# The x products on 64 by 64 tiles of TensorE, with heads and w_in rows rearranged, in a linear attention + snake MLP kernel

## The chip, the cores and the metric

The program runs on one NeuronCore of one Trainium2 chip. The metric is device time in microseconds (us), the median of three runs. One run under the profiler shows where the time lies. PE is TensorE (its weight loads are shown apart as PEld), DVE is VectorE, ACT is ScalarE, POOL is GpSimd, SP is SyncE, which issues most transfers. Times in the text without a unit are us.

## The reference

Eight batches, 8 heads, 576 positions, head size 64. Per batch and head:

```
q_s = softmax(q over its 64 columns)       k_s = softmax(k over the 576 positions)
kv  = k_s^T v          (64 x 64)
x   = q_s kv           (576 x 64), heads side by side: x is 4608 x 512
h   = x w_in           (4608 x 2048)
g   = h + sin(alpha h)^2 / alpha
out = g w_out          (4608 x 512)
```

Inputs and output are float32; all products run in bfloat16 with float32 sums in PSUM.

## The kernel before, in words

**Layouts.** A position of a batch is p*9 + j with 64 values p and J = 9 values j, and a column block (b, j) is 64 positions wide. Heads sit as h = 2i + e: i is 0 to 3 (i = 2*ii + x), e is 0 or 1. `ke` and `vb` hold e on the partition half; `qT` (transposed softmaxed q) holds for each ii the two heads x on the two partition halves. The kv product (`kv_mm`, line 174) is already made of 64 by 64 pieces: 64 rows of the array by 64 columns, 72 matmuls of 65 columns a batch (the 65th column is the softmax sum), which leaves heads x on the partition halves of PSUM tile `kvp`. `kv_norm` (184 to 188) divides by the sum and writes `kbd`, a 128 by 128 block diagonal matrix for each (e, ii) with zeros off the diagonal: two DVE instructions, one for each half.

**x products.** x is made transposed, as `xT`: 4 chunks of 128 rows by a ring of 2560 columns. One full 128 by 128 matmul with `kbd` (lines 223 and 231) makes one chunk c = 2*ii + e, of which only the diagonal blocks do work. So a batch takes 4 chunks times 576 columns.

**The MLP.** The 4608 columns are cut into 9 tiles t of 512. `mm_h` (254) makes the first product for 128 of the 2048 hidden rows at a time (16 blocks ni, 4 matmuls of 512 columns each); `sine` (260, 262 or 264, 266) squares the sine on ACT, POOL or DVE; `combine` (270, DVE) writes g. `mm_o` (274) is the second product: 4 row groups j of 16 matmuls of 512 columns, each group evacuated by DVE (286) and stored.

**PSUM.** Eight banks: two rotating `a`, two rotating `b`; later a pool `ps_o` of two and `ps_a` of two adjoining banks (one tile, for kv and x). A tile's first products use `aabb` four times over.

**Order.** It is written out by hand, engine by engine; every engine runs its own instructions in the order of the program. Tiles 0 to 2 have orders of their own (lines 361 to 595). In tiles 3 to 6 the batch b = t + 1 is prepared: ACT starts the tile with four exponentials of b (with a table load before and after), 8 second products of tile t - 1 go to PE, and then for each ni: `mm_h`, at ni = 3 the transposes by DMA and the loads of batch b + 1 on SP's queue, at ni = 5 the kv product, at ni = 9, 11, 13, 15 one pair of x products each into `ps_a` with one DVE copy each, then sine, combine and so many second products of tile t - 1 that `want` is reached. Tiles 7 and 8 interleave four second products with each block.

Of the kernel before, what the change touches and what calls it, by code (L numbers as in the profile page):

```python
# [15 lines left out]
F32 = mybir.dt.float32  # L16
# [7 lines left out]
def kernel(  # L24
# [20 lines left out]
    J = 9  # L45
# [26 lines left out]
    alpha_rows = singles.tile([nN, 128], F32, name="alpha_rows")  # L72
    alpha_sb = singles.tile([128, nN], F32, name="alpha_sb")
    inva_sb = singles.tile([128, nN], F32, name="inva_sb")
    kbd = [singles.tile([128, 2, 2, 128], BF16, name=f"kbd{n}") for n in range(2)]
    vb = [singles.tile([128, J, 4 * 65], BF16, name=f"vb{n}") for n in range(2)]

    def src_view(t, b):
        return t[b].rearrange("(i e) (p j) d -> (e p) i (j d)", e=2, j=J)

    win_v = moe_w_in.rearrange("(x c d) n -> x d c n", x=2, c=4)
    wout_v = moe_w_out.rearrange("(no ni) d -> ni no d", ni=128)
    out_v = out.rearrange("(b p j) d -> b j p d", b=B, j=J)

# [94 lines left out]
    def kv_norm(b, i0=0, i1=2):  # L179

        kt, m = kbd[b % 2], i1 - i0
        kvr = small.tile([128, 2, 2], F32, name="kvr")[:, :, 0:m]
        src = A["kvp", b][:, :, i0 * 65:i1 * 65].rearrange("p e (ii c) -> p e ii c", ii=m)
        nc.vector.reciprocal(kvr, src[:, :, :, D])
        for x in range(2):
            r = slice(64 * x, 64 * x + 64)
            nc.vector.tensor_tensor(kt[r, :, i0:i1, r], src[r, :, :, 0:D],  # L187
                                    kvr[r].unsqueeze(3).to_broadcast([64, 2, m, D]), op=ALU.mult)

    def q_tile(b):  # L190
        if ("qT", b) not in A:
# [23 lines left out]
    XO = ((0, 4), (4, 9))  # L215

    def attn_out(b, ii, half, pool, eng):
        qT, kt = A["qT", b], kbd[b % 2]
        j0, j1 = XO[half]
        n = (j1 - j0) * P  # L220
        xp = pool.tile([128, 2, 512], F32, name="xp", tag="a")
        for e in range(2):
            nc.tensor.matmul(xp[:, e, 0:n], kt[:, e, ii], qT[:, ii, j0:j1, e * 64:(e + 1) * 64],  # L223
                             start=True, stop=True)
        c0 = (J * b + j0) * P % NX
        eng(xT[:, 2 * ii:2 * ii + 2, c0:c0 + n], xp[:, :, 0:n])  # L226

    def attn_chunk(b, c, j0, j1, xp):

        ii, e = divmod(c, 2)  # L230
        nc.tensor.matmul(xp, kbd[b % 2][:, e, ii], A["qT", b][:, ii, j0:j1, e * 64:(e + 1) * 64],
                         start=True, stop=True)


    G = {}

    HP = {}
    BANKS = {0: "aabbkllaabbkllaa", 1: "kbbllaakbbllaabb", 2: "aabbooaabbooaabb"}

    def bank(kind):  # L240

        if kind == "k":
            return ps_k.tile([128, 2, MF], F32, name="kvp", tag="a")[:, 0]
        pool = {"a": lambda: ps_h[0], "b": lambda: ps_h[1], "l": lambda: ps_l, "o": lambda: ps_o}[kind]()
        return pool.tile([128, MF], F32, name={"l": "lp", "o": "op"}.get(kind, "hp"), tag=kind)

    def mm_h(t, ni, k0=0, k1=4):

        if ni == 0 and k0 == 0:
            G[t] = gpool.tile([128, nN, MF], BF16, name="g")  # L250
        hp = HP[t, ni] if k0 else bank(BANKS.get(t, 4 * "aabb")[ni])
        HP[t, ni] = hp
        for ki in range(k0, k1):
            nc.tensor.matmul(hp, win[:, ki, ni * 128:(ni + 1) * 128],  # L254
                             xT[:, ki, t * MF % NX:t * MF % NX + MF], start=(ki == 0), stop=(ki == 3))
        return hp

    def sine(t, ni, hp, sq):
# [48 lines left out]
    zero = singles.tile([128, 1], F32, name="zero")  # L307
    nc.vector.memset(zero, 0.0)
    for n in range(2):
        nc.vector.memset(kbd[n], 0.0)  # L310
        nc.vector.memset(vb[n].rearrange("p j (i c) -> p j i c", i=4)[:, :, :, D:D + 1], 1.0)

    ps_h = [ctx.enter_context(tc.tile_pool(name=f"ps_{n}", bufs=2, space=PSUM, reuse_waits="tile")) for n in "ab"]
# [63 lines left out]
    kv_norm(0, 0, 1)  # L377
    tp1 = ps_l.tile([128, 8, 128], BF16, name="tp", tag="l")
    q_transpose_ii(0, 1, 0, 8, tp1)
    cast_v0(1, 0, 5, ACT_CP)  # L380
    cast_v0(1, 5, 9, DVE_CP)

    xp = [bank("b") for _ in range(2)]
    for c in range(2):
        attn_chunk(0, c, 0, 8, xp[c])
    DVE_CP(xT[:, 0, 0:MF], xp[0])
    ACT_CP(xT[:, 1, 0:MF], xp[1])
    ACT_CP(A["qT", 0][:, 1, 0:8], tp1)
    nc.scalar.activation(zero, zero, AX.Sin)
    kv_mm(0, 1, ps_k, split=True)  # L390
# [1 line left out]
    for ki in range(2):  # L392
        for ni in range(2):
            mm_h(0, ni, ki, ki + 1)
    for c in range(2, 4):
        xp = bank("l")
        attn_chunk(0, c, 0, 8, xp)
        DVE_CP(xT[:, c, 0:MF], xp)
    for ki in range(2):
        for ni in range(2, 4):  # L400
            mm_h(0, ni, ki, ki + 1)
# [21 lines left out]
    def take(it, n=1000):  # L423
        for _ in range(n):
            if next(it, 0) == 0:
                return
# [4 lines left out]
    with ES:  # L431
# [47 lines left out]

        def x_half(ii):  # L480
            xp = [bank("a") for _ in range(2)]
            for e in range(2):
                attn_chunk(1, 2 * ii + e, 0, 8, xp[e])
            for e in range(2):
                (ACT_CP, DVE_CP)[e](xT[:, 2 * ii + e, MF:2 * MF], xp[e])

        kv_mm(1, 0, ps_k, split=True)
        kv_norm(1, 0, 1)
# [23 lines left out]
        def late_q8(ni):  # L512
            if ni == 11:
                tp = ps_k.tile([128, 2, 2, 128], BF16, name="tp", tag="a")
                for b in range(2):
                    for ii in range(2):
                        nc.tensor.transpose(tp[:, ii, b], A["qe", 1][:, J - 2 + b, ii * 128:(ii + 1) * 128], identb)
                DVE_CP(A["qT", 1][:, :, J - 2:J], tp)
            elif ni == 15:
                xp = ps_k.tile([128, 4, 2, P], F32, name="xp", tag="a")  # L520
                for c in range(4):
                    ii, e = divmod(c, 2)
                    for b in range(2):
                        nc.tensor.matmul(xp[:, c, b], kbd[b][:, e, ii],
                                         A["qT", 1][:, ii, J - 2 + b, e * 64:(e + 1) * 64], start=True, stop=True)
                DVE_CP(xT[:, :, 16 * P:18 * P], xp.rearrange("p c b n -> p c (b n)"))

        for ni in range(nN):
            h_slot(1, ni, SQ[ni], lag)
# [2 lines left out]
        cast_v(2, [GP_CP, GP_CP])  # L532
        flush(lag, 0)

    ps_o = ctx.enter_context(tc.tile_pool(name="ps_o", bufs=2, space=PSUM, reuse_waits="tile"))
    ps_a = ctx.enter_context(tc.tile_pool(name="ps_a", bufs=1, space=PSUM, reuse_waits="tile"))


    def o_stream(t, eng=DVE_CP):
        for j in range(4):  # L540
            acc = ps_o.tile([128, dm], F32, name="op", tag="o")
# [21 lines left out]
    norm_q(3, [GP])  # L563
    take(os, 20)

    c0 = J * 2 * P
    for c in range(4):
        xp = bank("aabb"[c])[:, 0:6 * P]
        attn_chunk(2, c, 0, 6, xp)
        (ACT_CP, DVE_CP)[c % 2](xT[:, c, c0:c0 + 6 * P], xp)  # L570
        take(os, 3 if c == 1 else 1)
    xp = ps_a.tile([128, 2, 512], F32, name="xp", tag="a")[:, :, 0:6 * P]
    for c in range(4):
        attn_chunk(2, c, 6, 9, xp[:, c // 2, (c % 2) * 3 * P:(c % 2 + 1) * 3 * P])
    DVE_CP(xT[:, :, c0 + 6 * P:c0 + 9 * P].rearrange("p (h c) n -> p h c n", h=2),
           xp.rearrange("p h (c n) -> p h c n", c=2))
    take(os)
    q_transpose_dma(3)
    load_batch(4)

    def attn_back(b, n, engs=4 * (DVE_CP,), xs=(4, 6, 8, 10)):
        if n == 0:
            kv_mm(b, 0, ps_a)
            kv_mm(b, 1, ps_a)
            kv_norm(b)
        elif n in xs:
            m = xs.index(n)
            attn_out(b, m // 2, m % 2, ps_a, engs[m])

    SQ2 = "PAPPAPAPPAPAPPAP"  # L590
    for ni in range(nN):
        h_slot(2, ni, SQ2[ni], lag)
        flush(lag, 2)
        attn_back(3, ni - 5, (DVE_CP, ACT_CP, ACT_CP, DVE_CP), (4, 6, 8, 10))
    flush(lag, 0)

    for t in range(3, nT):
        b = t + 1 if t + 1 < B else None
        os = o_stream(t - 1)
        done = 0  # L600
# [58 lines left out]
```

## Time and profile before

| | |
|---|---|
| median of 3 runs | 284.34 (284.31 to 284.47) |
| the profiled execution, its own time | 283.85 |
| its span, first to last instruction | 282.1 |
| granted PE clock, mean | 0.997 |
| PE busy | 270.1 (96%) |
| ACT busy | 225.5 (80%) |
| DVE busy | 188.7 (67%) |
| POOL busy | 83.8 (30%) |
| DMA | 45.80 MB, mean 162 GB/s |

A matmul's row shows its latency (379 ns for 512 columns); matmuls overlap, and in a stream they start 0.2157 apart (16 of them take 3.45 in the chain of waits). In the tables "idle before" is time in which the engine had nothing to run before a group, and behind the arrow stands what ended it. Some matmul records are missing from a trace: where a hole of one whole step stands in a regular stream, it is a missing record.

### The profile page before, as it was taken

The page shows a single profiled execution, that of the slowest core. Times are in us where ns is not written, and L with a number is a line of the kernel's source. Part 1 is how long each engine was busy: PE and PEld are TensorE (multiplying, and loading weights), DVE is VectorE, ACT ScalarE, POOL GpSimd, SP SyncE. Part 2 cuts the span into 40 slices and gives each one's busy share as a digit, 9 for nine tenths or more (in the row PEclk, how much of TensorE's full clock was granted, in tenths as well). Part 3 has the DMA queues.
Part 4 walks back from the last instruction along what each step waited for, and adds up shares of the span by engine and source line. Part 5 has one row for each costly group of instructions (what it writes and reads, how often), then busy time and mean ns, then how long its engine had stood idle before and what let it go on. Part 6 is the DMA issues. An engine that isn't in the chain of part 4 may idle for free.

```text
span 282.1 us, 4812 instructions
## 1 busy us (share of the span) xinstructions
PE 270.1 (96%) x1826; PEld 128.0 (45%) x1855; DVE 188.7 (67%) x288; ACT 225.5 (80%) x322; POOL 83.8 (30%) x80
## 2 busy tenths in 40 slices
PE   1999999999999999999999999999999999999994
PEld 0444444444444444444444444444444444444443
DVE  3968768899967768766875677567775555555412
ACT  3989576999589999899989998999877777777400
POOL 1988421877676550115003500340000000000000
PEclk9999999999999999999999999999999999999998
DMA  7999999996599039811992099109011111111143
GB/s 252 310 173 221 280 332 322 358 345 243 124 224 393 10 68 329 305 37 38 266 386 50 22 283 388 27 18 160 6 34 37 37 40 37 37 38 43 42 104 74
DMA packets 39127, 45.80 MB, mean 162 GB/s; under 512 B 17072, under 2 KB 22464, under 8 KB 39104
## 3 DMA queue, kind: packets, MB, share of 16 engines
q1 hardware_dynamic: 33360, 40.57, 46.9%
q0 software_dynamic: 5552, 4.79, 10.4%
q8 instruction: 14, 0.23, 0.3%
q10 hardware_dynamic: 192, 0.14, 0.2%
q14 instruction: 9, 0.07, 0.1%
HBM read 36.71 MB, written 9.44 MB: 164 GB/s over the span
## 4 chain that ended last, share of the span: by engine, by line
PE 84%; DMA 6%; ACT 3%; DVE 2%; POOL 1%; issue 1%; SPq 1%; ACTq 0%
PE op L274 38%; PE hp L254 37%; DMA st_v<-in_v_dram 6%; PE xp L223 2%; PE kvp L174 2%; PE lp L254 2%; POOL s L264 1%; PE op L629 1%; PE op L254 1%; ACT s L260 1%; PE kvp L254 1%; ACT vb L329 1%; DVE g L270 1%; SPq L299 1%; SPq L445 0%
## 5 line engine op out<-in xcount | busy, mean ns | idle before, releaser
L270 DVE SCALAR_TENSOR_TENSOR g<-s,inva_sb,hp 128x512 bf16<-128x512 f32 x128 | 94.1, 745 | 58.1 <-ACT s L262 52.6
L254 PE MATMUL hp<-xT,win 128*128 128x512 bf16 x507 | 127.9, 379 | 0.4
L274 PE MATMUL op<-wout,g 128*128 128x512 bf16 x477 | 121.6, 379 | 1.4 <-issue 0.6
L260 ACT ACTIVATE s<-hp,alpha_sb 128x512 f32<-128x512 f32 x128 | 86.3, 682 | 22.9 <-PE hp L254 21.2
L254 PEld LDWEIGHTS <-win 128*128 128x128 bf16 x576 | 56.0, 98 | 67.5 <-issue 1.3
L274 PEld LDWEIGHTS <-g 128*128 128x128 bf16 x560 | 54.0, 98 | 61.0 <-DVE g L270 0.3
L262 ACT ACTIVATE s<-s 128x512 f32<-128x512 f32 x112 | 70.5, 630 | 3.5
L264 POOL TENSOR_TENSOR s<-s 128x512 f32<-128x512 f32 x29 | 30.4, 1063 | 20.0 <-ACT s L260 19.9
L153 POOL TENSOR_TENSOR qn<-qe,qs 128x1152 bf16<-128x1152 bf16 (+1 forms) x12 | 25.1, 2109 | 34.1 <-DVE qs L147 22.7
L286 DVE COPY o<-op 128x512 f32<-128x512 f32 (+2 forms) x33 | 22.1, 668 | 9.9 <-PE op L274 5.5
L138 POOL CAST vb<-st_v 128x1152 bf16<-128x1152 f32 x12 | 14.7, 1257 | 45.3 <-DMA st_v<-in_v_dram 45.3
L119 ACT ACTIVATE qe<-st_q 128x1152 bf16<-128x1152 f32 (+2 forms) x18 | 17.7, 1025 | 6.7 <-DMA st_q<-in_q_dram 6.6
L119 ACT ACTIVATE ke<-st_k 128x1152 bf16<-128x1152 f32 x16 | 17.9, 1151 | 1.2 <-DMA st_k<-in_k_dram 1.2
L146 DVE TENSOR_REDUCE qs<-qe 128x36 f32<-128x2304 bf16 x5 | 12.8, 2553 | 7.9 <-ACT qe L119 7.9
L226 DVE CAST xT<-xp 128x512 bf16<-128x512 f32 (+1 forms) x18 | 13.5, 749 | 0.0
L119 ACT ACT_TABLE_LOAD x7 | 9.0, 1283 | 1.3 <-PEq L643 1.2
L274 PE MATMUL lp<-wout,g 128*128 128x512 bf16 x31 | 8.8, 379 | 0.2 <-issue 0.2
L274 PE MATMUL hp<-wout,g 128*128 128x512 bf16 x30 | 8.6, 379 | 0.1
L223 PE MATMUL xp<-qT,kbd 128*128 128x256 bf16 (+1 forms) x40 | 8.2, 286 | 0.0
L174 PEld LDWEIGHTS <-ke 64*64 64x64 bf16 x576 | 5.8, 108 | 4.6 <-ACT ke L119 0.8
L187 DVE TENSOR_TENSOR kbd<-kvp,kvr 64x256 bf16<-64x256 f32 (+1 forms) x20 | 7.4, 369 | 0.5
L254 PE MATMUL lp<-xT,win 128*128 128x512 bf16 x30 | 7.5, 379 | 0.1
(86 smaller groups left out, 135.0 us busy)
## 6 DMA issues: line engine op xcount, KB each, us to landing
out_dram<-o SPq DMA_DIRECT2D x70, 128.0 KB, 2.4
st_q<-in_q_dram SPq DMA_DIRECT2D x6, 1152.0 KB, 6.7
st_k<-in_k_dram SPq DMA_DIRECT2D x6, 1152.0 KB, 8.8
st_v<-in_v_dram SPq DMA_DIRECT2D x6, 1152.0 KB, 11.4
st_k<-in_k_dram SPq DMA_DIRECT2D x4, 576.0 KB, 7.5
st_q<-in_q_dram SPq DMA_DIRECT2D x4, 512.0 KB, 6.1
st_v<-in_v_dram SPq DMA_DIRECT2D x3, 576.0 KB, 8.0
wout<-in_moe_w_out_dram POOLq DMA_DIRECT2D x3, 512.0 KB, 10.3
```

Source lines behind the costliest of these rows:

```text
L119: nc.scalar.activation(dst[:, :, ii * 128:(ii + 1) * 128].rearrange("p j (x d) -> p x j d", x=2), src[:, ii::2], AX.Exp)
L138: engs[ii](vv[:, 2 * ii:2 * ii + 2, :, 0:D], staged["v", b][:, ii::2])
L153: engs[ii % len(engs)].tensor_tensor(qn[:, ii, 0:j1].rearrange("p j (x d) -> p j x d", x=2), qe[:, ii], part.unsqueeze(3).to_broadcast([12 ...
L223: nc.tensor.matmul(xp[:, e, 0:n], kt[:, e, ii], qT[:, ii, j0:j1, e * 64:(e + 1) * 64], start=True, stop=True)
L226: eng(xT[:, 2 * ii:2 * ii + 2, c0:c0 + n], xp[:, :, 0:n])
L254: nc.tensor.matmul(hp, win[:, ki, ni * 128:(ni + 1) * 128], xT[:, ki, t * MF % NX:t * MF % NX + MF], start=(ki == 0), stop=(ki == 3))
L260: nc.scalar.activation(s, hp, AX.Sin, scale=alpha_sb[:, ni:ni + 1])
L262: nc.scalar.activation(s, s, AX.Square)
L264: nc.gpsimd.tensor_tensor(s, s, s, op=ALU.mult)
L270: nc.vector.scalar_tensor_tensor(G[t][:, ni], in0=s, scalar=inva_sb[:, ni:ni + 1], in1=hp, op0=ALU.mult, op1=ALU.add)
L274: nc.tensor.matmul(acc, G[t][:, ni, j * 128:(j + 1) * 128], wout[:, ni, :], start=(ni == 0), stop=(ni == nN - 1))
L286: eng(o[:, cols], acc)
```

## The change

1. `kbd` keeps the 64 by 64 blocks alone, without zeros: `kv_norm` needs one DVE instruction on 128 partitions instead of two on 64, and the two clearing instructions at the start fall away.
2. An x product is four matmuls on 64 by 64 tiles (row half x, column half e) in place of two full ones. A chunk of `xT` now holds the two heads e of one (x, ii): chunk 2x + ii. Rows of w_in are permuted to match by the view that loads them, and `mm_h` runs over the chunks in the order 0, 2, 1, 3.
3. A batch's first 8 column blocks go as 512 columns; the ninth (`last_j`) goes apart: for batches 3 to 6 inside the next batch's kv product, in spare columns of its PSUM tile.
4. Batches 4 to 7: all x products at ni = 12 in one group, on four banks (one of `a`, one of `ps_o`, the two of `ps_a`), with copies at ni = 12, 13 and 14. For batch 3 two groups, at ni = 9 and 13, all copies on DVE. `ps_o` becomes two pools of one bank, and blocks 12 to 15 of a tile go `abba`.
5. In tiles 3 to 6, 17 second products instead of 8 go ahead of block 0, and `want` follows another line.
6. At the start ACT and DVE swap their parts of one cast of v.

```diff
-    kbd = [singles.tile([128, 2, 2, 128], BF16, name=f"kbd{n}") for n in range(2)]
+    kbd = [singles.tile([128, 2, 2, D], BF16, name=f"kbd{n}") for n in range(2)]
...
-    win_v = moe_w_in.rearrange("(x c d) n -> x d c n", x=2, c=4)
+    win_v = moe_w_in.rearrange("(c x d) n -> x d c n", x=2, c=4)
...
-        for x in range(2):
-            r = slice(64 * x, 64 * x + 64)
-            nc.vector.tensor_tensor(kt[r, :, i0:i1, r], src[r, :, :, 0:D],
-                                    kvr[r].unsqueeze(3).to_broadcast([64, 2, m, D]), op=ALU.mult)
+        nc.vector.tensor_tensor(kt[:, :, i0:i1], src[:, :, :, 0:D],
+                                kvr.unsqueeze(3).to_broadcast([128, 2, m, D]), op=ALU.mult)
...
+    def attn_x(b, ii, j0, j1, outs):
+
         for e in range(2):
-            nc.tensor.matmul(xp[:, e, 0:n], kt[:, e, ii], qT[:, ii, j0:j1, e * 64:(e + 1) * 64],
-                             start=True, stop=True)
+            for x in range(2):
+                r = slice(64 * x, 64 * x + 64)
+                nc.tensor.matmul(outs[x][64 * e:64 * e + 64], kbd[b % 2][r, e, ii],
+                                 A["qT", b][r, ii, j0:j1, e * 64:(e + 1) * 64], start=True, stop=True)
...
+    def x_copy(eng, c, b, xp):
+
+        n0 = min(8 * P, NX - J * b * P % NX)
+        for n, m in ((0, n0), (n0, 8 * P)):
+            if n < m:
+                d0 = (J * b * P + n) % NX
+                eng(xT[:, c, d0:d0 + m - n], xp[..., n:m])
+
+    def last_j(b, xn):
+
+        for ii in range(2):
+            attn_x(b, ii, J - 1, J, [xn[:, x, ii * P:(ii + 1) * P] for x in range(2)])
...
+    KO = (0, 2, 1, 3)
...
-        hp = HP[t, ni] if k0 else bank(BANKS.get(t, 4 * "aabb")[ni])
+        hp = HP[t, ni] if k0 else bank(BANKS.get(t, 3 * "aabb" + "abba")[ni])
...
-        nc.vector.memset(kbd[n], 0.0)
...
-    cast_v0(1, 0, 5, ACT_CP)
-    cast_v0(1, 5, 9, DVE_CP)
+    cast_v0(1, 0, 5, DVE_CP)
+    cast_v0(1, 5, 9, ACT_CP)
...
-    ps_o = ctx.enter_context(tc.tile_pool(name="ps_o", bufs=2, space=PSUM, reuse_waits="tile"))
+    ps_o = [ctx.enter_context(tc.tile_pool(name=f"ps_{n}", bufs=1, space=PSUM, reuse_waits="tile")) for n in "op"]
...
+    for ii in range(2):
+        xp = [bank("ab"[ii]) for _ in range(2)]
+        attn_x(2, ii, 0, 8, xp)
+        if ii == 1:
+            xn = ps_a.tile([128, 2, 512], F32, name="xp", tag="a")
+            last_j(2, xn)
+        for x in range(2):
+            x_copy((ACT_CP, DVE_CP)[x], 2 * x + ii, 2, xp[x])
+        take(os, 4)
+    last_j_copy(2, xn)
...
+    def x_pair(b, ii):
+        xp = ps_a.tile([128, 2, 512], F32, name="xp", tag="a")
+        attn_x(b, ii, 0, 8, [xp[:, x] for x in range(2)])
+        return xp
+
+    def attn_kv(b):
+
+        kv_mm(b, 0, ps_a)
+        kv_mm(b, 1, ps_a)
+        if b > 3:
+            xn = A["kvp", b][:, :, 256:512]
+            last_j(b - 1, xn)
+        kv_norm(b)
+        if b > 3:
+            last_j_copy(b - 1, xn)
...
-        attn_back(3, ni - 5, (DVE_CP, ACT_CP, ACT_CP, DVE_CP), (4, 6, 8, 10))
+        if ni == 5:
+            attn_kv(3)
+        elif ni in (9, 13):
+            ii = ni // 12
+            x_copy(DVE_CP, slice(ii, 4, 2), 3, x_pair(3, ii))
...
-            take(os, 8)
-            done = 8
+            take(os, 17)
+            done = 17
...
-                attn_back(b, ni - 5)
+                if ni == 5:
+                    attn_kv(b)
+                elif ni == 12:
+                    xl = [bank("a"), bank("o")]
+                    attn_x(b, 1, 0, 8, xl)
+                    xa = x_pair(b, 0)
+                    x_copy(DVE_CP, 1, b, xl[0])
+                elif ni == 13:
+                    x_copy(DVE_CP, 3, b, xl[1])
+                elif ni == 14:
+                    x_copy(DVE_CP, slice(0, 4, 2), b, xa)
+                if b == B - 1 and ni == 9:
+                    xn = ps_a.tile([128, 2, 512], F32, name="xp", tag="a")
+                    last_j(b, xn)
+                    last_j_copy(b, xn)
...
-            want = 23 + 2 * (t == 3) + 21 * ni // 8 if b is not None else 4 * (ni + 1)
+            want = 25 + (t == 3) + 5 * ni // 2 if b is not None else 4 * (ni + 1)
...
-        acc = ps_o.tile([128, dm], F32, name="op", tag="o")[:, 0:c1 - c0]
+        acc = bank("po"[c0 > 0])[:, 0:c1 - c0]
```

Batches 0 and 1 use `attn_x` in the places where they used the full matmuls, with chunks 2x + ii; the ninth blocks of both, which tile 1 makes together at its block 15 (line 524), take 16 small matmuls in place of 8.

More of the change, by code (lines that the diff above doesn't have):

```diff
@@ L213, in q_transpose_dma, with x_cols, last_j_copy @@
             nc.sync.dma_start(out=out, in_=in_, transpose=True)
[L215 to L221, printed above, removed]
-        for e in range(2):
-            nc.tensor.matmul(xp[:, e, 0:n], kt[:, e, ii], qT[:, ii, j0:j1, e * 64:(e + 1) * 64],
-                             start=True, stop=True)
-        c0 = (J * b + j0) * P % NX
[L226 to L232, printed above, removed]
+    def attn_x(b, ii, j0, j1, outs):
+        for e in range(2):
+            for x in range(2):
+                r = slice(64 * x, 64 * x + 64)
+                nc.tensor.matmul(outs[x][64 * e:64 * e + 64], kbd[b % 2][r, e, ii],
+                                 A["qT", b][r, ii, j0:j1, e * 64:(e + 1) * 64], start=True, stop=True)
+    def x_cols(b, j0, j1):
+        c0 = (J * b + j0) * P % NX
+        return slice(c0, c0 + (j1 - j0) * P)
+    def x_copy(eng, c, b, xp):
[7 more added lines that the diff above has]
+            attn_x(b, ii, J - 1, J, [xn[:, x, ii * P:(ii + 1) * P] for x in range(2)])
+    def last_j_copy(b, xn):
+        DVE_CP(xT[:, :, x_cols(b, J - 1, J)].rearrange("p (x i) n -> p x i n", x=2),
+               xn[:, :, 0:2 * P].rearrange("p x (i n) -> p x i n", i=2))
+    KO = (0, 2, 1, 3)
     G = {}
     HP = {}
-    BANKS = {0: "aabbkllaabbkllaa", 1: "kbbllaakbbllaabb", 2: "aabbooaabbooaabb"}
+    BANKS = {0: "aabbkllaabbkllaa", 1: "kbbllaakbbllaabb", 2: "aabbopaabbopaabb"}
     def bank(kind):
@@ L243, in bank @@
             return ps_k.tile([128, 2, MF], F32, name="kvp", tag="a")[:, 0]
-        pool = {"a": lambda: ps_h[0], "b": lambda: ps_h[1], "l": lambda: ps_l, "o": lambda: ps_o}[kind]()
-        return pool.tile([128, MF], F32, name={"l": "lp", "o": "op"}.get(kind, "hp"), tag=kind)
+        pool = {"a": lambda: ps_h[0], "b": lambda: ps_h[1], "l": lambda: ps_l, "o": lambda: ps_o[0], "p": lambda: ps_o[1]}[kind]()
+        return pool.tile([128, MF], F32, name={"l": "lp", "o": "op", "p": "op"}.get(kind, "hp"), tag=kind)
     def mm_h(t, ni, k0=0, k1=4):
@@ L250, in mm_h @@
             G[t] = gpool.tile([128, nN, MF], BF16, name="g")
-        hp = HP[t, ni] if k0 else bank(BANKS.get(t, 4 * "aabb")[ni])
+        hp = HP[t, ni] if k0 else bank(BANKS.get(t, 3 * "aabb" + "abba")[ni])
         HP[t, ni] = hp
-        for ki in range(k0, k1):
-            nc.tensor.matmul(hp, win[:, ki, ni * 128:(ni + 1) * 128],
-                             xT[:, ki, t * MF % NX:t * MF % NX + MF], start=(ki == 0), stop=(ki == 3))
+        for k in range(k0, k1):
+            nc.tensor.matmul(hp, win[:, KO[k], ni * 128:(ni + 1) * 128],
+                             xT[:, KO[k], t * MF % NX:t * MF % NX + MF], start=(k == 0), stop=(k == 3))
         return hp
@@ L379 @@
     q_transpose_ii(0, 1, 0, 8, tp1)
-    cast_v0(1, 0, 5, ACT_CP)
-    cast_v0(1, 5, 9, DVE_CP)
+    cast_v0(1, 0, 5, DVE_CP)
+    cast_v0(1, 5, 9, ACT_CP)
     xp = [bank("b") for _ in range(2)]
-    for c in range(2):
-        attn_chunk(0, c, 0, 8, xp[c])
+    attn_x(0, 0, 0, 8, xp)
     DVE_CP(xT[:, 0, 0:MF], xp[0])
-    ACT_CP(xT[:, 1, 0:MF], xp[1])
+    ACT_CP(xT[:, 2, 0:MF], xp[1])
     ACT_CP(A["qT", 0][:, 1, 0:8], tp1)
@@ L394 @@
             mm_h(0, ni, ki, ki + 1)
[L395 to L398, printed above, removed]
+    xp = [bank("l") for _ in range(2)]
+    attn_x(0, 1, 0, 8, xp)
+    for x in range(2):
+        DVE_CP(xT[:, 2 * x + 1, 0:MF], xp[x])
     for ki in range(2):
@@ L481, in x_half @@
             xp = [bank("a") for _ in range(2)]
[L482 to L485, printed above, removed]
+            attn_x(1, ii, 0, 8, xp)
+            for x in range(2):
+                (ACT_CP, DVE_CP)[x](xT[:, 2 * x + ii, MF:2 * MF], xp[x])
         kv_mm(1, 0, ps_k, split=True)
@@ L519, in late_q8 @@
             elif ni == 15:
-                xp = ps_k.tile([128, 4, 2, P], F32, name="xp", tag="a")
-                for c in range(4):
-                    ii, e = divmod(c, 2)
+                xp = ps_k.tile([128, 2, 512], F32, name="xp", tag="a")
+                for ii in range(2):
                     for b in range(2):
-                        nc.tensor.matmul(xp[:, c, b], kbd[b][:, e, ii],
-                                         A["qT", 1][:, ii, J - 2 + b, e * 64:(e + 1) * 64], start=True, stop=True)
-                DVE_CP(xT[:, :, 16 * P:18 * P], xp.rearrange("p c b n -> p c (b n)"))
+                        for e in range(2):
+                            for x in range(2):
+                                r, c = slice(64 * x, 64 * x + 64), (2 * ii + b) * P
+                                nc.tensor.matmul(xp[64 * e:64 * e + 64, x, c:c + P], kbd[b][r, e, ii],
+                                                 A["qT", 1][r, ii, J - 2 + b, e * 64:(e + 1) * 64],
+                                                 start=True, stop=True)
+                DVE_CP(xT[:, :, 16 * P:18 * P].rearrange("p (x i) n -> p x i n", x=2),
+                       xp[:, :, 0:4 * P].rearrange("p x (i n) -> p x i n", i=2))
         for ni in range(nN):
@@ L540, in o_stream @@
         for j in range(4):
-            acc = ps_o.tile([128, dm], F32, name="op", tag="o")
+            acc = bank("op"[j % 2])
             for ni in range(nN):
@@ L564 @@
     take(os, 20)
[L566 to L576, printed above, removed]
+    for ii in range(2):
+        xp = [bank("ab"[ii]) for _ in range(2)]
[3 more added lines that the diff above has]
+            last_j(2, xn)
+        for x in range(2):
+            x_copy((ACT_CP, DVE_CP)[x], 2 * x + ii, 2, xp[x])
+        take(os, 4)
+    last_j_copy(2, xn)
     take(os)
@@ L579 @@
     load_batch(4)
[L581 to L588, printed above, removed]
+    def x_pair(b, ii):
[11 more added lines that the diff above has]
+            last_j_copy(b - 1, xn)
     SQ2 = "PAPPAPAPPAPAPPAP"
```

## The prediction

> **What bounds the kernel now.** I read the page's busy rows first, then the chain that ended last, then what PE waits for, then its order of time, stage by stage.
>
> ```profile
> PE 270.1 (96%) x1826; PEld 128.0 (45%) x1855; DVE 188.7 (67%) x288; ACT 225.5 (80%) x322; POOL 83.8 (30%) x80
> ...
> PE 84%; DMA 6%; ACT 3%; DVE 2%; POOL 1%; issue 1%; SPq 1%; ACTq 0%
> ```
>
> Busy matmuls can hide idle time (a row lasts 379 ns, its place in a stream 216 ns), so PE's waits must be seen. All that are named, apart from the transpose of alpha at the start:
>
> ```profile
> PE warm L343 <- ACT qe L119: 1.6, 1, 1.6
> PE op L274 <- issue: 0.6, 4, 0.2
> PE kvp L174 <- ACT vb L329: 0.3, 1, 0.3
> PE lp L274 <- issue: 0.2, 1, 0.2
> ```
>
> From about 16 to 279 us PE has no hole but switches, missing records and a few tenths. So a matmul step less is worth its whole length, as long as ACT keeps up. Stage by stage (us, PE, PEld, DVE, ACT, POOL, clock, DMA), the window of one middle tile:
>
> ```profile
> 149.40:178.80 29.40, 29.14 (x207) 13.88 (x209) 20.49 (x30) 27.28 (x39) 7.45 (x5) 1.00 0.56 177
> ```
>
> ACT's rows overlap a little: its chain in a tile is 6.9 (two table loads, four exponentials) and 16 blocks by 1.24, so 26.8. PE can lose up to 2.5 of its 29.4 before ACT ends last. The clock is full, and nothing here changes that.
>
> **What a 64 by 64 matmul costs.** No row shows one of 512 columns, but kv's have the same tiles in the same order. PE's order of time in tile 2, with the full x products of batch 3 behind:
>
> ```profile
> 63.76 3.40 PE L274 MATMUL op<-wout,g 128*128 128x512 bf16 x15
> 67.09 0.81 PE L174 MATMUL kvp<-vb,ke 64*64 64x65 bf16 x72
> 67.82 4.49 PE L274 MATMUL op<-wout,g 128*128 128x512 bf16 x19
> ...
> 85.41 1.89 PE L254 MATMUL op<-xT,win 128*128 128x512 bf16 x8
> 87.28 0.43 PE L223 MATMUL xp<-qT,kbd 128*128 128x320 bf16 x2
> 87.55 1.89 PE L254 MATMUL hp<-xT,win 128*128 128x512 bf16 x8
> 89.32 0.38 PE L223 MATMUL xp<-qT,kbd 128*128 128x256 bf16 x2
> 89.54 1.89 PE L254 MATMUL hp<-xT,win 128*128 128x512 bf16 x8
> ```
>
> The 15 full matmuls end their places at 63.76 + 15 x 0.2157 = 67.00; kv starts at 67.09. Entering the small tiles costs 0.09. The 72 have a latency of 0.21, so their starts span 0.60, 8.3 ns each, against 65/2.4 = 27 ns for one that streams alone: 3.3 run side by side, at the full rate each. The last starts at 67.68 and the full ones resume at 67.82: 0.14, of which 0.03 is streaming, so leaving costs 0.11. A kv block is 0.83 in all.
>
> A group of four 512-column matmuls is then 0.09 + 0.01 (starts) + 0.22 + 0.11 = 0.43. The two full ones that it replaces are 2 x 0.2157 = 0.43: alone, it gains nothing. Two in one visit cost 0.65; eight ninth-block matmuls behind kv, with the switch already paid, 8 x 8.3 ns = 0.07. The gain can come only from sharing switches. Bounds for the unknown width: four wide (as above), or two wide (0.22 more for each four); kv's 3.3 is far nearer four.
>
> **A rule against it.** The Trainium skill, "TensorE: Matmul & The Clock Gate", Part 3 (Measured speedup vs the span model), gives 3.07 times for four row tiles of 512 columns. By it each four would take 4 x 0.216 / 3.07 = 0.28 instead of 0.23, an estimate, and 14 fours would lose 0.7 of the sum below; no row of this trace has such a matmul.
>
> **The sum, part by part** (PE's path, negative is a gain).
>
> Start: ACT's chain into the second x group is cast, xT copy, qT copy:
>
> ```profile
> 12.42 0.72 ACT L329 CAST vb<-st_v 128x640 bf16<-128x640 f32 x1
> 13.04 0.58 ACT L387 CAST xT<-hp 128x512 bf16<-128x512 f32 x1
> 13.51 1.02 ACT L388 COPY qT<-tp 128x1024 bf16<-128x1024 bf16 x1
> ```
>
> The swap gives ACT 512 elements instead of 640: by the slope between 640 (722 ns) and 1152 (1168 ns) 0.11 less, if the later half of v has landed. DVE's cast of it ran at 12.31, before ACT needs it. DVE's longer part and its xT copy fit, as `kbd` takes one instruction of 0.29 less there. Then PE waits for DVE's two copies as before (it waited till 16.35). **-0.11**; bounds 0 and -0.3.
>
> Batch 1: two lone groups, 0.43 against 0.43, **0**; the first waits 0.1 for `kbd` today, but the transposes after it wait for a copy, which eats that. The ninth blocks of batches 0 and 1: 8 full ones of 64 columns take 0.34 now (59.74 to 60.08); 16 small ones 0.09 + 0.13 + 0.14 = 0.36, **+0.03**. Batch 2: 0.98 now (four of 384 columns, four of 192); 0.43 + 0.43 + 0.07 = 0.93, **-0.05**.
>
> Batch 3: eight full ones of 256 and 320 columns, 2304/2.4 and 2.5 ns each = 0.98, and two waits in the fence above: eight matmuls from 85.41 end at 87.14, x starts at 87.28; from 87.55 at 89.28, x at 89.32. These 0.19 are the wait for the one `ps_a` tile to be copied; two groups four blocks apart have time. Now 0.43 + 0.43 + 0.07 (ninth block): **-0.24**. DVE takes all copies, two of 1024 elements, by the slope of 768 (947 ns) over 512 (683 ns) 1.21 each, against two of 0.68 and 0.82; kv_norm gives 0.43 back. It has 3 us of idle time there. But with 17 second products ahead the sixteenth comes 15 x 0.216 = 3.2 after the tile's last first product, 19 steps (4.1) before, and needs the last combine (94.81 before, I make it 94.4 against a start at 94.45): **+0.05**, bounds 0 and 0.3.
>
> Batches 4 to 6: 0.98 now; 0.65 + 0.07: -0.26 each, **-0.78**. Batch 7: its ninth block has no kv to ride on and pays a visit of its own, 0.09 + 0.06 + 0.14 = 0.29; 0.65 + 0.29 against 0.98, **-0.03**.
>
> New wait: at ni = 12 the second bank is `ps_o`'s first, which holds second products 33 to 48. The 48th is reached at ni = 10, and its copy stands behind combine 10 on DVE:
>
> ```profile
> 172.47 0.75 DVE L270 SCALAR_TENSOR_TENSOR g<-s,inva_sb,hp 128x512 bf16<-128x512 f32 x1 [0.77 <-ACT s L262]
> 173.13 0.68 DVE L286 COPY o<-op 128x512 f32<-128x512 f32 x1
> ```
>
> That copy ends 173.81, 2.92 after block 10's products (about 170.89). In the new order block 12 ends 13 steps (2.80) after block 10, the entry adds 0.09, and a signal to PE about 0.05: PE waits some 0.07, and behind it the whole queue of PE waits. **+0.2** for tiles 4 to 6 (tile 3 has one more product ahead and reaches the 48th at ni = 9); bounds 0 and 0.5 each if DVE runs late.
>
> Costed at nothing: the copies at ni = 12 to 14 (0.68, 0.68, 1.21) lie on DVE, which is 70% busy; combine 12 comes about 0.8 later, combine 14 about 1.3, and the next user of each bank and the sixteenth second product follow by 2 us or more. Batch 4's columns cross the end of the ring, so its copies are six of about 0.4 to 0.7: 0.4 more, same cover. Block 15 takes block 12's bank: 4.1 after it, its combine done by 2.3. Tile 7's block 15 frees a bank for tile 8's block 1: 12 steps (2.59) against sine, square and combine (2.3), slack 0.2. Block 4 needs combine 0, whose sine waits for the exponentials: 10.6 after the last block, PE comes at 11.2 (52 steps), about the same slack as before, when x at ni = 15 stood there. The evacuation of second products 1 to 16 now goes ahead of combine 0 on DVE, while DVE waits for the exponentials' squares. SP's queue keeps its order, and POOL's loads of w_in have the same sizes and count; the rows come from other places only. The clearing of `kbd` (two of 0.27) stood before a DVE wait of 1.9.
>
> Sum: -0.11 + 0.03 - 0.05 - 0.24 + 0.05 - 0.78 - 0.03 + 0.2 = **-0.93**. The profiled execution, 283.85 with 1.75 around its span, would be 282.9. It lies 0.5 under the median of 284.34; against that the forecast is **283.4**. A measurement tells 0.2% (0.57) from no change.
>
> **Rivals.**
>
> *The waits eat it.* The `ps_o` bank and the sixteenth second product: at 0.25 instead of 0.07 in three tiles and 0.2 behind tile 2 there is 0.7 more, and the time is 284.1, within 0.2%. For it: these two margins are the smallest, under 0.1. Against: DVE idles about 9 us of a tile, so delays don't add up.
>
> *Small matmuls of 512 columns are narrower or leave later* (the other side). Two wide: 14 fours by 0.22 is +3.0, so 286.4. If leaving waits for the whole latency (379 ns in place of 216), 0.16 in 10 visits (two each in batches 1, 2 and 3, one each in 4 to 7) is +1.6: 285.0. It decides from 0.07 more per four. For it: no such row. Against: kv runs at 8.3 ns a matmul, and entering kv behind full 512-column matmuls costs only 0.09 past their streaming.
>
> *The gain is larger.* No wait at `ps_o`, none behind tile 2, 0.1 at the first group of batch 1, 0.2 more at the start: -1.5, 282.8. For it: PE idles 1.4 us between 11.9 and 16.4. Against: each of those holes ends with an ACT or DVE step that the change hardly shortens.
>
> **How the numbers follow.** Forecast (-0.6 to -1.3, so 283.0 to 283.75) 0.56; larger gain 0.08; waits eat it 0.20; narrow or late tiles 0.16. Faster by over 0.2% is the forecast and the larger gain, 0.64; the same 0.2; slower 0.16, all of it from the last. The range goes from the larger gain, 282.8, to 285.1, which takes in part of the late tiles and leaves two-wide out.
>
> **What would show it.** Right: the lone x group replaces a stretch of 0.43 by one of about 0.43; the pair of groups at ni = 12 takes 0.65 beyond its neighbours' steps; tiles 4 and 5 take 29.1 instead of 29.4; batch 3's x starts without a wait. Wrong: four x matmuls whose starts are more than 20 ns apart, a resume over 0.35 after the last of them, PE or PEld waiting for `o` L286 or for `g` L270 at the head of a tile, or tiles still of 29.4.

## The result, and the profile after

The changed kernel takes 283.42 us (median of 9 runs) beside 284.31 of the kernel before (9 runs). The ratio, which is taken over all the runs and not from the medians, is 0.9973, 95% interval 0.996 to 0.9986: faster, though the interval leaves open whether by more than 0.2%. A second comparison, told at the end of the experiments, gave 0.9975 (0.9965 to 0.9986). The forecast was 283.4. The profiled execution took 283.53, its span is 281.7.

The page's busy rows and its chain, of the changed kernel:

```profile
PE 268.6 (95%) x1890; PEld 124.2 (44%) x1919; DVE 185.4 (66%) x280; ACT 224.1 (80%) x320; POOL 83.5 (30%) x80
...
PE 85%; DMA 5%; DVE 4%; ACT 2%; issue 2%; POOL 1%; SPq 0%; ACTq 0%
```

PE is still the bound and is busy for 1.5 less. Its main waits after the warm-up, summed over the span:

```profile
PE op L283 <- issue: 1.1, 7, 0.2
PE kvp L174 <- ACT vb L474: 0.8, 1, 0.8
PE hp L263 <- DVE kvr L184: 0.3, 1, 0.3
PE kvp L174 <- DVE vb L337: 0.2, 1, 0.2
```

One is new and large: 0.8 at the first kv product of batch 1 (line 174), which waits for ACT's cast of its v. It and the two waits for DVE lie ahead of 41 us; the seven of `op` are holes of one step (0.2157) each, missing records. Where PE's time went behind 41 us is seen in windows from one batch's kv product to the next (us, then busy time of PE, PEld, DVE, ACT, POOL, clock, DMA share, GB/s). Before, tiles 4 and 5:

```profile
133.38:162.83 29.45, 29.19 (x208) 13.93 (x210) 20.62 (x30) 27.56 (x40) 6.48 (x4) 1.00 0.62 179
162.83:192.25 29.42, 29.16 (x208) 13.87 (x210) 20.51 (x30) 27.30 (x39) 6.47 (x4) 1.00 0.56 177
```

After, the same two:

```profile
133.65:162.93 29.28, 28.91 (x214) 13.37 (x216) 20.18 (x29) 27.31 (x40) 6.48 (x4) 1.00 0.58 178
162.93:192.18 29.25, 28.88 (x214) 13.33 (x217) 20.09 (x29) 27.13 (x39) 6.48 (x4) 1.00 0.56 178
```

Each is 0.17 shorter. In one profile of each kernel, from the first kv product of batch 1 to the end, before takes 242.24 and after 241.47: 0.77 less. Ahead of it the changed kernel's profiled execution lost 0.42 (its kv product starts at 40.25 instead of 39.83), so the spans differ by 0.35 alone; the medians differ by 0.89. The first 40 us vary from execution to execution, as the experiments show.

**The small tiles.** A visit is a stretch in which PE works on the 64 by 64 tiles, between full matmuls. PE's order of time in tile 2, after:

```profile
81.32 0.84 PE L174 MATMUL kvp<-vb,ke 64*64 64x65 bf16 x72
82.09 3.63 PE L263 MATMUL hp<-xT,win 128*128 128x512 bf16 x15
85.65 0.41 PE L218 MATMUL xp<-qT,kbd 64*64 64x512 bf16 x4
85.99 1.90 PE L263 MATMUL op<-xT,win 128*128 128x512 bf16 x8
87.73 1.89 PE L263 MATMUL hp<-xT,win 128*128 128x512 bf16 x8
89.55 0.41 PE L218 MATMUL xp<-qT,kbd 64*64 64x512 bf16 x4
89.89 1.90 PE L263 MATMUL hp<-xT,win 128*128 128x512 bf16 x8
```

The eight first products from 87.73 end their places at 87.73 + 8 x 0.2157 = 89.46. The four small matmuls start at 89.55, all within 0.01, and the full ones go on at 89.89: 0.43 for the visit, as forecast, and the same as two full matmuls of 512 columns. They run four side by side. Both x visits of batch 3 start without a wait; before, 0.14 and 0.05 stood there.

The one visit of tile 4, for batch 5 (a hole of one step before 145.14 is a missing record):

```profile
143.31 1.03 PE L263 MATMUL hp<-xT,win 128*128 128x512 bf16 x4
144.27 0.40 PE L218 MATMUL hp<-qT,kbd 64*64 64x512 bf16 x1
144.36 0.37 PE L218 MATMUL op<-qT,kbd 64*64 64x512 bf16 x1
144.36 0.40 PE L218 MATMUL hp<-qT,kbd 64*64 64x512 bf16 x1
144.37 0.40 PE L218 MATMUL op<-qT,kbd 64*64 64x512 bf16 x1
144.51 0.47 PE L218 MATMUL xp<-qT,kbd 64*64 64x512 bf16 x4
145.14 0.59 PE L283 MATMUL op<-wout,g 128*128 128x512 bf16 x2 [0.16 <-issue]
```

The second matmul, into ps_o's bank (`op`), starts 0.09 after the first. DVE in the same stretch:

```profile
142.96 0.75 DVE L279 SCALAR_TENSOR_TENSOR g<-s,inva_sb,hp 128x512 bf16<-128x512 f32 x1 [0.55 <-ACT s L271]
143.62 0.69 DVE L295 COPY o<-op 128x512 f32<-128x512 f32 x1
```

The copy that frees the bank ends at 144.31, and 0.05 later the matmul starts: the wait that was forecast at 0.07. The prediction named starts more than 20 ns apart as a sign of being wrong. They are that far apart here, but through this one wait: in both visits of tile 2, and in this visit where the pair with `op` goes second (below), four start within 11 ns.

### The profile page after: what moved, and what is told of

Its sections match the earlier page's. It is cut to its first block, busy times and chain, and to the rows that moved or that the text cites. A ratio compares the mean times of both kernels' runs of the same rounds, so it can differ in the third digit from the quotient of the medians.

```text
span 281.7 us, 4930 instructions
## 1 busy us (share of the span) xinstructions
PE 268.6 (95%) x1890; PEld 124.2 (44%) x1919; DVE 185.4 (66%) x280; ACT 224.1 (80%) x320; POOL 83.5 (30%) x80
## 4 chain that ended last, share of the span: by engine, by line
PE 85%; DMA 5%; DVE 4%; ACT 2%; issue 2%; POOL 1%; SPq 0%; ACTq 0%
PE op L283 38%; PE hp L263 37%; DMA st_v<-in_v_dram 3%; PE kvp L174 2%; PE lp L263 2%; DMA st_q<-in_q_dram 1%; POOL s L273 1%; PE op L263 1%; PE op L663 1%; ACT s L269 1%; PE hp L218 1%; PE kvp L263 1%; DVE qs L364 1%; DVE qn L366 1%; PE xp L218 1%
## 5 line engine op out<-in xcount | busy, mean ns | idle before, releaser
L283 PEld LDWEIGHTS <-g 128*128 128x128 bf16 x560 | 53.2, 98 | 64.7 <-issue 2.3
L119 ACT ACTIVATE qe<-st_q 128x1152 bf16<-128x1152 f32 (+2 forms) x18 | 17.7, 1024 | 6.2 <-DMA st_q<-in_q_dram 6.0
L174 PE MATMUL kvp<-vb,ke 64*64 64x65 bf16 x576 | 6.9, 194 | 1.1 <-ACT vb L474 0.8
L109 POOL DMA_DIRECT2D win<-in_moe_w_in_dram x12 | 7.4, 701 | 0.0
L231 DVE CAST xT<-xp 128x1024 bf16<-128x1024 f32 (+1 forms) x7 | 7.4, 1065 | 0.0
```

What stands on the lines that cost most here:

```text
L119: nc.scalar.activation(dst[:, :, ii * 128:(ii + 1) * 128].rearrange("p j (x d) -> p x j d", x=2), src[:, ii::2], AX.Exp)
L174: nc.tensor.matmul(kvp[64 * x:64 * x + 64, e, ii * 65:(ii + 1) * 65], ke[r, j, h * 64:(h + 1) * 64], vt[r, j, h * 65:(h + 1) * 65], start= ...
L283: nc.tensor.matmul(acc, G[t][:, ni, j * 128:(j + 1) * 128], wout[:, ni, :], start=(ni == 0), stop=(ni == nN - 1))
```

## The experiments

The theory: PE's work is the bound behind batch 1's loads; a visit costs 0.2 for entering and leaving, so that small tiles gain only where visits are shared. The rivals: the small tiles gain by themselves; the new order of second products gains; the start gains. Each run is told by its ratio to the kernel before on the same chip and by its stages from kv to kv.

**The old places.** Batches 3 to 7 on small tiles, with the ninth blocks in the visits, 8 second products ahead and `aabb` throughout.

```diff
+    XO = ((0, 4), (4, 9))
+
+    def x_part(b, n, engs=4 * (DVE_CP,)):
+        if n not in (4, 6, 8, 10):
+            return
+        m = (n - 4) // 2
+        ii, (j0, j1) = m // 2, XO[m % 2]
+        xp = ps_a.tile([128, 2, 512], F32, name="xp", tag="a")
+        w = (j1 - j0) * P
+        attn_x(b, ii, j0, j1, [xp[:, x, 0:w] for x in range(2)])
+        engs[m](xT[:, ii::2, x_cols(b, j0, j1)], xp[:, :, 0:w])
...
-                elif ni == 12:
-                    xl = [bank("a"), bank("o")]
-                    attn_x(b, 1, 0, 8, xl)
-                    xa = x_pair(b, 0)
...
+                x_part(b, ni - 5)
```

> The changed kernel with the x products of batches 3 to 7 back in the places of the kernel before (four visits of 256 or 320 columns a batch, ninth blocks in them, 8 second products ahead), but still on 64 by 64 tiles. Theory (a visit to the small tiles costs 0.19 for entering and leaving, and the gain is in sharing visits): a visit takes 0.33 (256 columns) or 0.36 (320) beyond its neighbours' steps, where the full matmuls took 0.22 and 0.27; 1.38 a batch instead of 0.98, so 0.40 more in each of five batches: about 286.2, some 2.0 slower than the kernel before. Rival (the small tiles themselves are the gain, wherever they stand): at or under 283.4.

Ratio 1.0077 (1.0043 to 1.0111) over five runs, by the medians 285.73 against 284.20. The profiled execution is the slowest of the five (288.12; clock 0.96 in its first 41.8 us, and the first kv product of batch 1 only at 41.81), so only its later stages are read. Tiles 4 and 5:

```profile
136.32:166.20 29.88, 29.61 (x214) 13.28 (x217) 20.28 (x29) 27.57 (x40) 6.48 (x4) 1.00 0.55 176
166.20:196.05 29.85, 29.59 (x214) 13.21 (x217) 20.12 (x29) 27.30 (x39) 6.48 (x4) 1.00 0.57 175
```

Each takes 0.43 more than with full matmuls; from batch 2's kv product to the end it is 216.93 against 214.99, 1.95 more, where 2.0 was forecast. Its PE order of time in tile 4:

```profile
142.99 0.30 PE L218 MATMUL xp<-qT,kbd 64*64 64x256 bf16 x4
143.22 0.60 PE L283 MATMUL op<-wout,g 128*128 128x512 bf16 x2
143.66 1.03 PE L263 MATMUL hp<-xT,win 128*128 128x512 bf16 x4
```

A visit of 256 columns ends 0.23 after its start, plus 0.09 of entry: 0.32 where two full matmuls took 0.22. The streaming halves, the switches cost more than that. The small tiles in the old places are a loss of 1.5 to 2 us; the first rival is out.

**Two visits.**

```diff
                     attn_x(b, 1, 0, 8, xl)
-                    xa = x_pair(b, 0)
                     x_copy(DVE_CP, 1, b, xl[0])
                 elif ni == 13:
+                    xa = x_pair(b, 0)
                     x_copy(DVE_CP, 3, b, xl[1])
```

> The changed kernel with the one visit of batches 4 to 7 parted: one pair of heads behind block 12, the other behind block 13. Theory: one more entry and exit a tile, 0.20 to 0.22 by four tiles, +0.85 against the changed kernel, so about 284.2, and tiles 4 and 5 take 29.45 from kv to kv instead of 29.25. Rival (the gain comes from fewer waits and the new order, not from shared visits): the same as the changed kernel, 283.4.

```profile
134.11:163.62 29.51, 29.24 (x214) 13.34 (x217) 20.18 (x29) 27.36 (x40) 6.47 (x4) 1.00 0.59 176
163.62:193.10 29.48, 29.22 (x214) 13.30 (x217) 20.09 (x29) 27.18 (x39) 6.48 (x4) 1.00 0.56 177
```

Tiles 4 and 5 take 29.51 and 29.48, 0.23 more each, and from the first kv product of batch 1 to the end it is 242.41, 0.94 more than the changed kernel and 0.17 more than the kernel before. The ratio is 1.0015 (0.9994 to 1.0036): the gain of the whole change is gone with this one shared visit a tile.

**Eight ahead.**

```diff
-            take(os, 17)
-            done = 17
+            take(os, 8)
+            done = 8
...
-            want = 25 + (t == 3) + 5 * ni // 2 if b is not None else 4 * (ni + 1)
+            want = 23 + 2 * (t == 3) + 21 * ni // 8 if b is not None else 4 * (ni + 1)
```

> The changed kernel with 8 instead of 17 second products ahead of block 0, and the old line of want. Theory (PE has work all the time, so the order of its work is worth nothing): within 0.2 of the changed kernel, no hole on PE at the head of a tile; tiles 4 and 5 29.2 to 29.3 from kv to kv. Rival (the 17 ahead cover a wait at the head of the tiles): 0.2 or more for each of four tiles, 284.2 or above, with a hole before block 4 that combine 0 ends.

Ratio 0.9981 (0.9965 to 0.9998). Tiles 4 and 5 are 29.28 and 29.25, as in the changed kernel, and from batch 1's first kv product to the end 241.59, 0.12 more. The second products handed over ahead are worth next to nothing, and 0.11 of the 0.12 stands in one place: at the head of tile 4 block 4 starts 0.32 after the matmul before it instead of 0.22, 0.05 after combine 0 has ended on DVE.

```profile
131.49 0.59 PE L283 MATMUL op<-wout,g 128*128 128x512 bf16 x2
132.03 1.02 PE L263 MATMUL hp<-xT,win 128*128 128x512 bf16 x4
131.23 0.75 DVE L279 SCALAR_TENSOR_TENSOR g<-s,inva_sb,hp 128x512 bf16<-128x512 f32 x1 [1.81 <-ACT s L271]
```

That is the hole that the rival named, in one of four tiles (0.03 in tile 3) and not 0.2 in each.

**The old shares of the cast.**

```diff
-    cast_v0(1, 0, 5, DVE_CP)
-    cast_v0(1, 5, 9, ACT_CP)
+    cast_v0(1, 0, 5, ACT_CP)
+    cast_v0(1, 5, 9, DVE_CP)
```

> The changed kernel with the old shares of the first cast of v (ACT 5 of 9, DVE 4 of 9). Theory A (the start is on the path): PE's last wait for xT at the start ends 0.1 later and the time is 0.1 longer. Theory B (whatever PE gains at the start is lost at its wait for batch 1's v near 40 us): the start is 0.1 later, the first kv product of batch 1 starts where it does in the changed kernel apart from what its loads vary, and the time is the same within 0.1.

Ratio 0.9975 (0.9958 to 0.9991), 283.51: no difference, though the 0.1 in question is less than these runs can show. The first kv product of batch 1 starts at 40.20 against 40.25, here without a wait. That fits theory B, but also a start that varies for other reasons.

**The own pair first.** The wait for ps_o's bank moved behind the pair that needs no foreign bank.

```diff
-                    attn_x(b, 1, 0, 8, xl)
                     xa = x_pair(b, 0)
+                    attn_x(b, 1, 0, 8, xl)
```

> The changed kernel, in the one visit of batches 4 to 7 the pair that goes into ps_a first and the pair that goes into the banks of a and ps_o second. Theory (the second matmul of the visit waits for the copy that frees ps_o's bank, about 0.08 in tiles 4 to 6): the wait goes, tiles 4 and 5 take 29.19 to 29.21 instead of 29.28 and 29.25 from kv to kv; the time is 0.2 shorter, hardly to be seen. Rival (the starts of the visit are spread by the weight loads of the second pair): 29.25 to 29.28 as before.

The visit of tile 4 in its trace:

```profile
142.72 1.03 PE L263 MATMUL hp<-xT,win 128*128 128x512 bf16 x4
143.67 0.41 PE L218 MATMUL xp<-qT,kbd 64*64 64x512 bf16 x4
143.91 0.38 PE L218 MATMUL hp<-qT,kbd 64*64 64x512 bf16 x1
143.91 0.38 PE L218 MATMUL op<-qT,kbd 64*64 64x512 bf16 x1
143.92 0.38 PE L218 MATMUL hp<-qT,kbd 64*64 64x512 bf16 x1
143.92 0.38 PE L218 MATMUL op<-qT,kbd 64*64 64x512 bf16 x1
144.46 0.59 PE L283 MATMUL op<-wout,g 128*128 128x512 bf16 x2 [0.16 <-issue]
```

The first four start within 0.01 of each other, the second four 0.24 later, again together. From the end of block 12 (143.58) to the missing step before 144.46 (144.24) the visit takes 0.66, forecast 0.65. Tiles 4 and 5 fall to 29.19 and 29.17, 0.08 each; the rival is out. Ratio 0.996 (0.9946 to 0.9974).

**Batch 1's loads earlier and later.** In tile 0 the loads hang on a block; the later one has 14 in place of 12.

```diff
-        late = {6: lambda: load_q1(0), 8: lambda: load_wout(8, 12), 10: lambda: load_wout(12, 14), 13: lambda: (load_q1(1), load_kv1())}
+        late = {6: lambda: load_q1(0), 8: lambda: load_wout(8, 12), 10: lambda: load_wout(12, 14), 12: lambda: (load_q1(1), load_kv1())}
```

> The changed kernel with batch 1's second half of q and its k and v loaded one block earlier in tile 0 (block 12 instead of 13). Theory B (PE's first kv product of batch 1, near 40 us, is set by the landing of v, so what PE gains at the start is lost there): ACT's cast of v comes up to 0.9 earlier, PE waits for nothing there, and the time is 0.2 to 0.8 shorter. Rival (the transfers share a full bus with w_out, so an earlier issue lands no earlier; or the wait of the profiled execution was chance): within 0.15 of the changed kernel.

> The same loads one block later (block 14). Theory B: the issue comes some 0.8 later and so does the first kv product of batch 1; the time is 0.6 to 0.9 longer. Rival (there is slack): under 0.2 longer.

Earlier: ratio 0.9961 (0.9942 to 0.998), median 282.57. Later: 0.9972 (0.9957 to 0.9987), median 282.70. The two medians, on one chip, are 0.13 apart; theory B put them 0.8 or more apart. In both, PE waits for nothing at batch 1's first kv product (39.31 and 39.34), and the rest is 241.48 and 241.45. ACT's cast of v in the changed kernel:

```profile
39.03 1.17 ACT L474 CAST vb<-st_v 128x1152 bf16<-128x1152 f32 x1 [1.21 <-DMA st_v<-in_v_dram]
```

and with the loads one block later:

```profile
37.76 1.17 ACT L474 CAST vb<-st_v 128x1152 bf16<-128x1152 f32 x1 [0.27 <-DMA st_v<-in_v_dram]
```

SP issued this v at 30.30 in the changed kernel and at 30.95 here; ACT could cast it 1.27 earlier for an issue 0.65 later. On the chip of this run the own pair first shows the same: issued at 30.24, cast from 38.48. With the loads one block earlier it was issued at 29.05 and cast from 38.09. So the landing doesn't follow the issue, and theory B, that the issue behind PE's own start sets it, fell. The wait of 0.8 in the changed kernel's profile is no lasting part of the change: its second profile (below) doesn't have it.

**Both.** The own pair first, and the loads at block 12.

```diff
-        late = {6: lambda: load_q1(0), 8: lambda: load_wout(8, 12), 10: lambda: load_wout(12, 14), 13: lambda: (load_q1(1), load_kv1())}
+        late = {6: lambda: load_q1(0), 8: lambda: load_wout(8, 12), 10: lambda: load_wout(12, 14), 12: lambda: (load_q1(1), load_kv1())}
...
-                    attn_x(b, 1, 0, 8, xl)
                     xa = x_pair(b, 0)
+                    attn_x(b, 1, 0, 8, xl)
```

> Both: batch 1's loads at block 12 and the ps_a pair first in the visit. Theory: the sum of the two, 0.4 to 1.0 under the changed kernel, 282.4 to 283.0. Rival (neither is on the path in most executions): 283.4.

Ratio 0.997 (0.9957 to 0.9982), and 241.17 from batch 1's first kv product on, as with the own pair alone (241.16). The median is 282.76, against 282.44 with the own pair alone and 282.57 with the loads alone: inside the range named, but no sum of two gains. The loads add nothing.

**Both kernels again, and w_in's rows alone.** Four runs on one chip. The open question was the start: PE waits 0.5 to 0.9 for w_in there in seven of the eleven profiles of the changed kernel and its variants, as here with the own pair first:

```profile
PE hp L263 <- DMA win<-in_moe_w_in_dram: 0.7, 1, 0.7
```

The kernel before, unchanged:

> The kernel before, unchanged, for a second profile of it beside the next three on one chip. From its first kv product of batch 1 to the end it should take 242.24 again, within 0.05, as every stage there is PE's own work; what varies lies ahead of it. If the start is set by the transfers (a full bus), its last wait for xT or w_in at the start lies anywhere between 16.1 and 17.5, as in the changed kernel's profiles; if the change made the start better or worse, this profile stands apart from theirs.

Ratio 0.9994 (0.9986 to 1.0003), median 283.31, 0.31 under the 283.62 that the same kernel took in the other runs of this chip, so a difference of 0.3 between medians tells little. The matmul that waited for xT till 16.35 in the first profile starts at 15.88 here, without a wait and ahead of the range named. PE has no wait for w_in on its list; one gap of 0.12, too short for the list, ends with it. From batch 1's first kv product to the end it is 242.09, 0.15 less than forecast, all of it in batch 1's own stage; from batch 2's kv product on it repeats the first profile's 214.99 to 0.003.

```diff
-    win_v = moe_w_in.rearrange("(x c d) n -> x d c n", x=2, c=4)
+    win_v = moe_w_in.rearrange("(c x d) n -> x d c n", x=2, c=4)
```

> The kernel before with the view of w_in's rows of the changed kernel and nothing else, so that rows of w_in meet the wrong rows of x: the same work on the wrong pairs. Theory C (w_in lands later by its new rows): its transfers take 5.6 to 6.0 (median) from issue to landing instead of 5.1, PE waits 0.5 to 0.9 for w_in in the start, and the time is 0.3 to 0.8 longer. Rival (the bus is full either way, and rows of the same length cost the same): landings and time like the kernel before's on this chip, within 0.2%.

Landing in 5.7 against 5.6 of the run above (medians of 12 transfers), no wait for w_in, ratio 0.9988 (0.9976 to 0.9999). The new rows cost nothing that shows; theory C fell too.

> The changed kernel again, beside the kernel before on one chip. Theory (the gain is 0.77 of PE work from the first kv product of batch 1 on, and the start gives nothing, as transfers set it): from there to the end 241.47 within 0.05, and 0.6 to 0.95 faster in all. Rival (the start gains 0.1 to 0.5 on top): 1.0 to 1.3 faster.

Ratio 0.9975 (0.9965 to 0.9986), 282.85: 0.77 less than the 283.62 of the kernel before on this chip, but only 0.46 less than the 283.31 of its runs just above. From batch 1's first kv product on it is 241.41, 0.68 under the kernel before's 242.09. From batch 2's kv product to the end, where the kernel before repeats itself, the gain is 0.76 (0.70 in the first pair of profiles). Before and after on this chip:

```profile
66.42:281.40 214.98, 209.87 (x1403) 100.22 (x1424) 136.94 (x196) 172.00 (x248) 44.40 (x31) 1.00 0.44 122
66.70:280.92 214.22, 208.78 (x1451) 96.50 (x1472) 135.19 (x194) 170.82 (x246) 44.91 (x31) 1.00 0.43 122
```

The first kv product of batch 1 starts at 39.52, against 39.32 in the kernel before and 39.22 with the new rows alone: ahead of it nothing is gained, and 0.2 to 0.3 lost in these profiles.

> The changed kernel with the ps_a pair first in the one visit of batches 4 to 7, again, beside the changed kernel on one chip: 0.2 to 0.3 faster than it (three waits of 0.08 for ps_o's bank), 241.2 from the first kv product of batch 1 to the end; 1.0 under the kernel before.

Ratio 0.9966 (0.9954 to 0.9979), 282.61 against 282.85, and 241.27. It is the lowest median on this chip. The medians' difference of 0.24 is what the stages of batches 5 to 7 say (0.08, 0.08 and 0.07 less); the whole stretch is 0.14 shorter, as batch 3's stage took 0.10 more in this profile. The intervals overlap: the stages show this gain, the times alone don't.

## Why the prediction was right, point by point

- *What bounds the kernel*: right. PE works without holes from batch 1 on, ACT's share of tiles 4 and 5 stayed at 27.1 to 27.6, and what PE's work lost behind the start, the time lost.
- *Entry 0.09, exit 0.11, four side by side; a lone visit gains nothing*: right, and shown twice, by the old places (lone short visits lose 0.43 a tile) and the two visits (0.23 for one visit more). The small rest is in the last section: the second full matmul behind a visit comes 0.01 late too. The Trainium skill's 3.07 times ("TensorE: Matmul & The Clock Gate", Part 3), by the prediction's estimate, would have made a four 0.28; with the own pair first the second four starts 0.24 after the first. So the measurement decides against that estimate; the page's row itself is for four row tiles, and no run here has those.
- *Start, -0.11*: the term that the runs don't bear out. The two pairs of profiles put the first kv product of batch 1 at 39.83 and 39.32 before, and at 40.25 and 39.52 after: 0.42 and 0.20 later, not earlier. The medians, less what the stages behind it gained, leave about 0.1 of gain there, which is less than medians of one kernel differ by (0.31). The old shares of the cast gave the same time. What PE waits for there changes from profile to profile: ACT's cast, DVE, or w_in (0.5 to 0.9 in seven profiles, one of them with the old shares, and none of that size in the three with the order of before). The profile of before showed ACT's chain as the last to end; that transfers stand close behind it was not priced. What sets their landing, and whether the new order meets w_in more often by itself or by chance, was not settled.
- *Batch 1 and its ninth blocks, 0 and +0.03*: 27.25 and 27.10 before (27.44 with the new rows), 27.19 and 27.19 after, so 0 within what it varies. *Batch 2, -0.05*: 13.91 to 13.88, -0.03.
- *Batch 3, -0.24, of which 0.07 of cost falls into the next stage*: 23.37 to 23.36 and 23.32 with one second product (0.22) more in the stage, so -0.23 to -0.27 against -0.31 for that part. Both waits went. *+0.05 behind it*: it was 0. Combine 15 ended at 94.80, the sixteenth second product started at 94.87: right that it is close.
- *Batch 4, -0.26*: 29.02 to 28.98 with one second product more: -0.25. *Batches 5 and 6, -0.26 and a wait of 0.07*: -0.17 each; with the own pair first -0.25. The sign of 29.1 for tiles 4 and 5 left that wait out: they took 29.28 and 29.25, and 29.19 and 29.17 with the own pair first. *Batch 7, -0.03 and the wait*: 89.83 to 89.55 with two second products fewer (0.43), so +0.15 for the visit of its own, the wait, and batch 6's ninth block: forecast +0.11.
- *The rest at nothing*: held. The pairs' copies of 1024 elements took 1.22 (estimate 1.21), and no bank was late but ps_o's. The one-instruction `kv_norm` and the new bank pools were not run alone; both are in the old places' run, which came within 0.05 of a forecast that gives them nothing.
- *The sum*: forecast -0.93, of which -0.82 behind the start; measured -0.77 and -0.68 there, and at the start nothing that could be told. So the mechanism is right and its size a little large. That the median of 283.42 meets 283.4 to 0.02 is luck: medians differ by 0.3 for one kernel, and the two comparisons gave 0.89 and 0.77. *The rivals*: late or narrow tiles are out; of the waits, ps_o's came at its forecast size and the other not at all.

## What to carry to other kernels

Price a switch of the array's tiling from a block that already has one, both ways, before moving a product to smaller tiles: here entry and exit together cost 0.2, as much as the smaller product saved, and only visits that hold twice the work, or that ride on another visit, gained. Put the matmuls that need a bank of a busy pool last in a shared visit. Where the start is full of transfers, don't book a shorter step on an engine as a gain until the transfer behind it has been priced as well; here the booked 0.11 could not be found.

## What the runs showed of the hardware

- Entering the 64 by 64 tiles costs the same in every visit behind the start: the first start comes 309 ns after that of the last full matmul, 93 more than a step of 216.
- Leaving, the next full matmul starts 332 ns after the last start of a lone four of 512 columns, 252 after that of a four of 320 and 225 of 256: 0.418 for each column and 118 fixed. Behind matmuls of 64 or 65 columns it is 123 to 145, behind the second four of a shared visit 308. The second full matmul then comes 227 behind the first, 11 more than a step.
- Between 24 and 40 us, where the transfers' share of the DMA engines is above 1 (1.14, 310 GB/s in the changed kernel's profile), a transfer issued later did not land later: 0.65 later was 1.27 earlier in one pair of executions, and 0.71 later was 0.72 earlier in a pair on one chip. The first 40 us of one kernel varied by 0.5 to 0.7 between its two profiles, while the stages from batch 2's kv product on repeated to a few hundredths.
